# Query features and x of three groups in full-depth matmuls with block diagonal matrices, and an earlier masked multiplication for z

## The chip, the cores and the metric

The kernel runs on one core of a Trainium2 chip. The metric is the device time of one execution in microseconds (us), as a median over runs. The engines are named as the profile does: PE is TensorE (matmuls), PEld its weight loads, DVE is VectorE, ACT is ScalarE, POOL is GpSimd, SP is SyncE, whose queue starts most of the DMAs.

## The reference, cut to what matters

```
def phi(x):                                   # r = 8
    a = einsum('rd,bhsd->bhsr', S1, x)
    b = einsum('rd,bhsd->bhsr', S2, x)
    return einsum('bhsi,bhsj->bhsij', a, b)   # 64 features
kv  = einsum('bhsf,bhsd->bhfd', phi(k), v)
z   = sum_s phi(k)
x   = (phi(q) @ kv) / (phi(q) . z + 1e-6)     # 4 batches, 4 heads, 1088 rows, 32 columns
x   = x transposed to (4352, 128)             # heads side by side
h   = x @ w_in                                # 128 -> 2048
g   = where(h > 0, h, exp(min(h, 0)) - 1)     # ELU
out = g @ w_out                               # 2048 -> 128
```

All is computed in fp32. The weights arrive as 64-bit words and are rounded on the chip.

## The kernel before, in words

The 4352 rows are cut into 9 groups: eight of 512 rows (two to a batch) and group 8, the last 64 rows of each of the four batches (256 rows). The groups 4 and 5, and 6 and 7, are handled as pairs up to x.

The order of all work is written out by hand. After an opening part, a loop runs over steps n = 2 to 63. A step belongs to a group and to one of eight pairs of 128-column blocks of the hidden layer. In it PE computes `h` (`mm1`, at L256: two blocks, 512 rows; up to step 29 each product is four matmuls that are 32 columns wide, from step 30 two that are 64 wide), ACT and DVE make the ELU of both blocks (`elu`: L808 and L810 on ACT, L816 on DVE), and PE runs the second product of step n-2 (L256 for group 0, L713 for most of group 1, and from step 16 on a scheme of seven products of quarter blocks at L737, for which POOL adds up ELU results at L696 to L701). Calls that are hung on a step by hand stand in lists: `at(n, ...)` after mm1 of step n, `mid(n, ...)` after the first block's ELU, `late(n, ...)` after the second's. Each engine works through its instructions in that order.

Hung on the steps are the key side of batches 1 to 3 and the query side of groups 2 to 8:

- `KF_late` (L359) computes the key features of a batch into two banks `kfps`, `KF_late_out` (L369) turns them, `KO_a` (L378) copies one factor to PSUM (tile `ka`) and `KO_b` (L386) multiplies, `KA` (L427) sums kv and z into one bank `kv`. `sums_out` copies z's part (`ZC`, L444) and turns kv (`KT_out`, L436), which stores it to DRAM and loads it back in four copies (`kvs`, L439 and L440). `turn` multiplies z's part with a matrix on PE (`Z`), `turned` multiplies it with a mask on DVE (`Z_out`, L453) and adds heads together on POOL (`Z_share`, L458 and L459) into `SWs`.
- `queries(g5, g1, n)` (L655) computes x of a group (`q5`, L642) and the features of a later one (`q1`, L536), in 32x32 tiles of the array: 16 matmuls for the features, two times 16 for x. They write four banks: the two `h` banks of the next step and two `aux` banks (`qps`). `q1_out` (L548) turns four pieces on DVE, `q5_out` (L653) copies four pieces on ACT. `q2_den` (L560 to L570) makes the quotient, `q2_half` (L625) the outer product, `q4` (L632) turns it.

PSUM has four banks for `h` (two steps), two for everything with the tag `aux`, used in turn, and one each for the two outputs. A tile with tag `aux` waits for the readers of the tile that had its bank.

```
    for n, g, nx in ((13, None, 2), (15, 2, 3), (22, 3, 4), (30, 4, 6), (46, 6, 8), (62, 8, None)):
        at(n, queries, g, nx, n + 1)
```

So x of group 3 and the features of group 4 stand in step 22, and so on. The key side of batch 2 has `KF_late` in step 16, `KA` in 19 and z in 20; that of batch 3 has `KF_late` in 21, `KO_b` in 23 and 24, `KA` in 27 and z in 28.

Of the kernel before, what the change touches and what calls it, by code (L numbers as in the profile page):

```python
# [12 lines left out]
F32 = mybir.dt.float32  # L13
# [9 lines left out]
def _ap(ap: bass.AP, free):  # L23
    return dataclasses.replace(ap, ap=[list(ap.ap[0])] + [list(x) for x in free])
# [3 lines left out]
def kernel(  # L28
# [21 lines left out]
    nc = tc.nc  # L50
    B, H, S, D = q.shape
    R = S1.shape[0]
    P = 128
    FD = H * D
# [3 lines left out]
    NT = S // 64  # L58
# [5 lines left out]
    const = ctx.enter_context(tc.tile_pool(name="const", bufs=1))  # L64
    work = ctx.enter_context(tc.tile_pool(name="wk", bufs=2))
    psum = ctx.enter_context(tc.tile_pool(name="psum", bufs=2, space=bass.MemoryType.PSUM))
# [6 lines left out]
    qT = [const.tile([FD, NT, 64], F32, name=f"qT{b}") for b in range(2)] * 2  # L73
    qE = const.tile([FD, 2, 64], F32, name="qE")
# [162 lines left out]
    bmask = const.tile([FD, H], F32, name="bmask")  # L237
# [15 lines left out]
    def quarters(dst, lhs, rhs, tile=None, **kw):  # L253
        tile = tile or width[0]
        for c in range(0, P, tile):
            nc.tensor.matmul(dst[c:c + tile], lhs[:, c:c + tile], rhs, skip_group_check=True,  # L256
                             tile_position=(0, c), **kw)
# [36 lines left out]
    Sab = const.tile([FD, H, 2 * R], F32, name="Sab")  # L294
    SW = const.tile([FD, H, 3, R], F32, name="SW")
# [16 lines left out]

    def make_SWs():
        nc.gpsimd.memset(SWs[:, :, 3, :], 0.0)
        for b in range(B):
            nc.gpsimd.tensor_add(SWs[:, b, :2, :], Sxp[:, :, 0, :], Sxp[:, :, 1, :])


# [5 lines left out]


    kvS = const.tile([P, H, D], F32, name="kvS")
    kvs = {b: const.tile([P, H, 2, D], F32, name=f"kvs{b}") for b in range(B)}
    dram = ctx.enter_context(tc.tile_pool(name="dram", bufs=1, space=bass.MemoryType.DRAM))
    kvd = {b: dram.tile([P, 2 * D], F32, name=f"kvd{b}")[:] for b in range(B)}
    kv_ps, feats, wzs, kf_ps = {}, {}, {}, []  # L330


# [99 lines left out]

    def KT_out(b):

        kt = work.tile([P, 2 * D], F32, name="kvt", tag="kvt")
        nc.vector.transpose(kt[:], kv_ps[b][:, :R * R])  # L436
        nc.sync.dma_start(kvd[b], kt[:])
        src = kvd[b].rearrange("(h p) x -> p h x", h=H)
        for w in range(4 if b else 1):  # L439
            nc.sync.dma_start(kvs[b][32 * w:32 * w + 32].rearrange("p h f d -> p h (f d)"), src)  # L440

    def ZC(b, ps):
        zl = work.tile([P, H * R], F32, name="zl", tag="zl")
        nc.scalar.copy(zl[:], ps[:, R * R:R * R + H * R])  # L444
        return zl
# [3 lines left out]
        quarters(ps[:, 96:128], SXh[:], zl[:], None if b else 64)  # L449

    def Z_out(b, ps):
        z = wzs[b] = SW[:, :, 2, :] if b == 0 else work.tile([FD, H, R], F32, name="wz", tag="wz")[:]
        nc.vector.tensor_mul(z, ps[:, 96:128].rearrange("p (h i) -> p h i", h=H), _ap(bmask[:], [[1, H], [0, R]]))  # L453

    def Z_share(b):
        z = wzs.pop(b)
        zh = work.tile([FD, 2, R], F32, name="zh", tag="zh")
        nc.gpsimd.tensor_add(zh[:], z[:, :2], z[:, 2:])  # L458
        nc.gpsimd.tensor_add(SWs[:, b, 2, :], zh[:, 0], zh[:, 1])  # L459
# [14 lines left out]
    NQ = (NH + 7) // 8  # L474
    qn = [min(8, NH - 8 * g) // 2 for g in range(NQ)]
    abw, ans, qp, qpT, xg, xps = {}, {}, {}, {}, {}, {}
# [7 lines left out]
    def half_tile(g, k):  # L484
        return (g // 2, 8 * (g % 2) + k) if g < NQ - 1 else (k, NT - 1)
# [36 lines left out]
    units = {g: ([g, g + 1] if 4 <= g < NQ - 1 else [g]) for g in [2, 3] + list(range(4, NQ, 2))}  # L522
    un = {g: sum(qn[x] for x in gr) for g, gr in units.items()}

    def quarter_of(g, w):

        n = un[g] // 2
        return (*half_tile(g + n * w // 8, n * w % 8), n)

    def q1(g, ps, o, opened):  # L530
        for w in range(4):
            b, t, n = quarter_of(g, w)
            qs = qE[:, b:b + 1, :] if g == NQ - 1 and b < 2 else qT[b][:, t:t + n, :]
            for r in range(4):
                rows = slice(32 * r, 32 * r + 32)
                nc.tensor.matmul(ps[r][32 * w:32 * w + 32, o:o + 64 * n], SWs[rows, b].rearrange("p x r -> p (x r)"),  # L536
                                 qs[rows].rearrange("p t s -> p (t s)"),
                                 start=not opened, stop=True, skip_group_check=True, tile_position=(32 * r, 32 * w))
        abw[g] = ps, o

    def q1_out(g):
        (ps, o), n = abw[g], un[g]
        pair = n > 4
        abw[g] = work.tile([P, H * n if pair else H * 4, 4 * R], F32, name="abw", tag="abwp" if pair else "abw",
                           bufs=1 if pair else 2)
        m = H * n // len(ps)
        for r in range(len(ps)):
            nc.vector.transpose(abw[g][:, m * r:m * r + m, :].rearrange("p m y -> p (m y)"),  # L548
                                ps[r][:, o:o + 32 * m])
# [97 lines left out]
    def q5_out(g, i=0):  # L647

        n = 32 * un[g]
        ps = xps[g] if len(units[g]) == 1 else xps[g][2 * i:2 * i + 2]  # L650
        x = xg[g + i] = work.tile([P, 512], F32, name="xg", tag="xg", bufs=3)
        for w in range(len(ps)):
            nc.scalar.copy(x[:, n * w:n * w + n], ps[w][:, :n])  # L653

    def queries(g5, g1, n):  # L655

        hs[steps[n]] = [psum.tile([P, 512], F32, name="h", tag="h", bufs=4) for c in range(2)]
        ps = hs[steps[n]] + [psum.tile([P, 512], F32, name="qps", tag="aux") for _ in range(2)]
        if g5 is not None:
            q5(g5, ps, 0)  # L660
        if g1 is not None:
            q1(g1, ps, 256 if g5 is not None else 0, g5 is not None)
        if g5 is not None:
            q5(g5, ps, 1)
# [236 lines left out]
    KO_first(5, 7)  # L901
    Z(0, zps, zl)
    Z_out(0, zps)
    KO_first(7, KT)
    keep_warm(1, 96, 64)
# [52 lines left out]
    def at(n, f, *a):  # L958
        extra.setdefault(n, []).append((f, *a))

    def mid(n, f, *a):
        extra.setdefault((n, 0), []).append((f, *a))

    def late(n, f, *a):
        extra.setdefault((n, 1), []).append((f, *a))
# [8 lines left out]
    late(3, keep_last, 0)  # L974
    late(14, keep_last, 1)
    late(2, make_SWs)
    late(3, Z_share, 0)
    late(3, KT_out, 0)
    zls = {}

    def sums_out(b):
        zls[b] = ZC(b, kv_ps[b])
        KT_out(b)
# [3 lines left out]

    def turned(b):
        Z_out(b, kv_ps[b])
        Z_share(b)  # L990


    for b, (n_t, n_f, n_o, n_a, n_z) in enumerate(
            ((4, 6, (7, 9), 11, 12), (15, 16, (17, 18), 19, 20), (19, 21, (23, 24), 27, 28)), 1):
        at(n_t, transp, kT, "k", b, 0, NT)
        at(n_f, KF_late, b)
        late(n_f, KF_late_out, b)
        for half in range(2):
            if b == 1:
                at(n_o[half], KO, b, half, nc.gpsimd)  # L1000
            else:
                late(n_o[half] - 1, KO_a, b, half)
                at(n_o[half], KO_b, b, half)
        at(n_a, KA, b)
        late(n_a, sums_out, b)
        at(n_z, turn, b)
        late(n_z, turned, b)
    late(10, transp, qT, "q", 1, 0, NT)
    at(21, transp, qT, "q", 2, 0, NT)
    late(24, transp, qT, "q", 3, 0, NT)  # L1010

    for n, g, nx in ((13, None, 2), (15, 2, 3), (22, 3, 4), (30, 4, 6), (46, 6, 8), (62, 8, None)):
        at(n, queries, g, nx, n + 1)
        if g is not None:
            mid(n, q5_out, g)
        if nx is not None:
            mid(n, q1_out, nx)
        if g is not None and len(units[g]) > 1:
            late(n, q5_out, g, 1)
# [3 lines left out]
    late(19, q2_den, 3)  # L1023
    late(19, q2_half, 3, 0)
    late(20, q4, 3)
    late(22, q2_den, 4)
    for n, g, i in ((25, 4, 0), (26, 4, 1), (32, 6, 0), (35, 6, 1)):
        late(n, q2_a, g, i)
    at(26, q2_half, 4, 0)
# [17 lines left out]
    for n in range(2, N):  # L1047
        g, cp = steps[n]
# [29 lines left out]
        g, cp = before  # L1078
# [10 lines left out]
    g = NQ - 2  # L1089
# [53 lines left out]
```

## Time and profile before

| | |
|---|---|
| median of 3 runs | 264.51 us (264.0 to 264.83) |
| span of the profiled execution | 262.8 us |
| what lies around the span, against the median | 1.7 us |
| PE busy | 256.6 us (98%) |
| DVE, ACT, POOL busy | 188.4, 183.0, 169.4 us |
| chain that ended last | PE 93% |
| x of a group and features (`h`, `qps` at L642, and `h` at L536), of the chain | 1.4%, 0.8%, 0.7% |

The span is the time from the first to the last instruction of one profiled execution. Times of single instructions are from that execution. The chain is followed back from the last instruction: at each step to what released it, or to the instruction before it on its engine. An instruction's row gives its start, its length, its engine and line, what it writes and reads and, in brackets, the idle time of the engine before it and what ended that. Lengths on one engine overlap a little: two DVE rows of 0.68 us take 1.27 us together.

### The profile page before, as it was taken

The numbers are of one execution on the slowest core, as the hardware profiler recorded it, in microseconds if no ns is written. First come the engines' busy times: TensorE is split into PE (matmuls) and PEld (weight loads), VectorE is DVE, ScalarE is ACT, GpSimd is POOL, SyncE is SP. The second block draws the span as 40 slices with busy tenths as digits, with TensorE's granted clock in tenths as the row PEclk, the third lists the DMA queues.
The fourth block names the chain that finished last, engine by engine and source line by source line (L and its number), as shares of the span: only waits on it lengthen the run. The fifth ranks groups of instructions, "written<-read, shape, count | busy, mean of one in ns | idle before, by whom it ended". The sixth has DMA issues, their size and how long they took to land.

```text
span 262.8 us, 9940 instructions
## 1 busy us (share of the span) xinstructions
PE 256.6 (98%) x4219; PEld 159.2 (61%) x4219; DVE 188.4 (72%) x355; ACT 183.0 (70%) x356; POOL 169.4 (64%) x253
## 2 busy tenths in 40 slices
PE   8899999999999999999999999999999999999994
PEld 6652333354446756667666666665666666667994
DVE  6799999997969997997477676644456445664651
ACT  2469878667567647785687777776777777777792
POOL 4420008204587996798868799898689888997310
PEclk9999999999999999999999999999999999999999
DMA  6999079012012220001100200011001100110021
GB/s 167 315 360 224 12 229 253 28 34 81 12 19 30 31 39 5 5 15 29 32 0 4 30 13 2 0 29 15 5 0 18 26 4 0 20 23 5 2 30 33
DMA packets 28507, 14.30 MB, mean 54 GB/s; under 512 B 21392, under 2 KB 26640, under 8 KB 28464
## 3 DMA queue, kind: packets, MB, share of 16 engines
q1 hardware_dynamic: 28032, 13.32, 21.2%
q8 instruction: 33, 0.54, 0.9%
q10 hardware_dynamic: 368, 0.30, 0.3%
q14 instruction: 10, 0.08, 0.1%
q0 software_dynamic: 64, 0.07, 0.1%
HBM read 11.31 MB, written 2.36 MB: 52 GB/s over the span
## 4 chain that ended last, share of the span: by engine, by line
PE 93%; DMA 2%; DVE 1%; ACT 1%; SPq 0%; issue 0%; DVEq 0%
PE h L256 44%; PE pb L737 16%; PE pa L737 13%; PE o L256 5%; PE pb L713 4%; PE ol L256 3%; DMA hd_q<-in_q_dram 2%; PE h L642 1%; PE kv L427 1%; PE kfps L359 1%; PE qps L642 1%; PE h L536 1%; PE qtp L595 1%; DVE qp L583 0%; PE xps L602 0%; PE qps L536 0%
## 5 line engine op out<-in xcount | busy, mean ns | idle before, releaser
L256 PE MATMUL h<-xg,W 128*32 128x512 f32 (+3 forms) x904 | 131.0, 540 | 0.4 <-ACT xg L608 0.4
L816 DVE SCALAR_TENSOR_TENSOR gg<-e,h 128x512 f32<-128x512 f32 x128 | 85.5, 681 | 54.2 <-ACT e L810 50.7
L808 ACT ACTIVATE e<-h 128x512 f32<-128x512 f32 x128 | 75.5, 590 | 47.4 <-PE h L256 46.5
L810 ACT ACTIVATE e<-e 128x512 f32<-128x512 f32 x128 | 80.9, 632 | 3.8
L256 PEld LDWEIGHTS h<-xg,W 128*32 128x32 f32 (+1 forms) x904 | 43.2, 122 | 43.1 <-issue 33.5
L699 POOL TENSOR_TENSOR tt<-gg 128x256 f32<-128x256 f32 x50 | 36.9, 738 | 15.6 <-DVE gg L816 15.2
L701 POOL TENSOR_TENSOR tt<-gg,tt 128x256 f32<-128x256 f32 x50 | 38.0, 761 | 3.9
L696 POOL TENSOR_TENSOR tt<-gg 128x256 f32<-128x256 f32 x50 | 36.7, 735 | 5.6 <-DVE gg L816 5.2
L700 POOL TENSOR_TENSOR tt<-tt,gg 128x256 f32<-128x256 f32 x50 | 36.6, 732 | 3.9
L737 PEld LDWEIGHTS pa<-gg,W 128*64 128x64 f32 (+1 forms) x496 | 24.0, 126 | 23.7 <-issue 23.0
L737 PE MATMUL pa<-gg,W 128*64 128x128 f32 (+1 forms) x496 | 30.7, 274 | 0.0
L737 PE MATMUL pb<-tt,SS 128*64 128x128 f32 (+1 forms) x480 | 29.7, 273 | 0.0
L737 PEld LDWEIGHTS pb<-tt,SS 128*64 128x64 f32 (+1 forms) x480 | 22.9, 126 | 0.0
L737 PE MATMUL pa<-tt,SS 128*32 128x128 f32 (+1 forms) x288 | 21.2, 273 | 0.0
L737 PE MATMUL pb<-tt,W 128*64 128x128 f32 (+1 forms) x256 | 20.2, 273 | 0.0
L737 PE MATMUL pb<-gg,SS 128*64 128x128 f32 (+1 forms) x256 | 20.0, 273 | 0.0
L134 POOL TENSOR_TENSOR raw<-raw,tiny 128x512 f32<-128x512 f32 x1 | 1.0, 1044 | 24.7 <-DVE raw L129 24.7
L256 PE MATMUL o<-gg,W 128*32 128x512 f32 x128 | 15.3, 595 | 0.0
L737 PEld LDWEIGHTS pa<-tt,SS 128*32 128x32 f32 (+1 forms) x288 | 13.8, 124 | 0.0
L737 PEld LDWEIGHTS pb<-tt,W 128*64 128x64 f32 (+1 forms) x256 | 12.9, 125 | 0.1
L737 PEld LDWEIGHTS pb<-gg,SS 128*64 128x64 f32 (+1 forms) x256 | 12.8, 125 | 0.0
L713 PE MATMUL pb<-gg,W 128*32 128x256 f32 x192 | 11.6, 380 | 0.0
(154 smaller groups left out, 285.0 us busy)
## 6 DMA issues: line engine op xcount, KB each, us to landing
raw<-in_moe_w_in_dram SPq DMA_DIRECT2D x8, 256.0 KB, 6.5
raw<-in_moe_w_out_dram SPq DMA_DIRECT2D x8, 256.0 KB, 6.6
out_dram<-ob SPq DMA_DIRECT2D x112, 16.0 KB, 1.5
hd_k<-in_k_dram SPq DMA_DIRECT2D x3, 544.0 KB, 7.6
hd_q<-in_q_dram SPq DMA_DIRECT2D x3, 544.0 KB, 8.8
v<-in_v_dram SPq DMA_DIRECT2D x4, 288.0 KB, 7.6
v<-in_v_dram SPq DMA_DIRECT2D x4, 256.0 KB, 8.9
kvs<-kvd SPq DMA_DIRECT2D x13, 32.0 KB, 2.0
```

The source lines that it names most:

```text
L256: nc.tensor.matmul(dst[c:c + tile], lhs[:, c:c + tile], rhs, skip_group_check=True, tile_position=(0, c), **kw)
L359: nc.tensor.matmul(ps[g2][32 * c:32 * c + 32, :32 * KT], Sxp[r].rearrange("p x c r -> p (x c r)"), kT[b][r, u * KT:u * KT + KT, 32 * w:32 ...
L642: nc.tensor.matmul(ps[w][32 * r:32 * r + 32, :64 * n], kvs[b][rows, r, f, :], qpT[g, i][rows, o:o + 2 * n, f, :], start=(f == 0), stop=(f ...
L696: nc.gpsimd.tensor_tensor(t[:, 0], b12, b11, op=SUB)
L699: nc.gpsimd.tensor_tensor(t[:, 2], b22, b12, op=SUB)
L700: nc.gpsimd.tensor_tensor(t[:, 1], t[:, 2], b11, op=ADD)
L701: nc.gpsimd.tensor_tensor(t[:, 3], b21, t[:, 1], op=SUB)
L713: nc.tensor.matmul(acc[1][0][r:r + width[0], 256 * hi:256 * hi + 256], lhs[:, w:w + width[0]], gg[:, c, 256 * u:256 * u + 256], start=(cp ...
L737: nc.tensor.matmul(bank[r:r + width[0], P * col:P * col + P], lhs[:, w:w + width[0]], rhs[:, u], start=(first and i in ((0,) if g == 1 els ...
L808: nc.scalar.activation(e, hs[g, cp][c][:, :n], RELU, scale=-1.0)
L810: nc.scalar.activation(e, e, EXP, scale=-1.0)
L816: nc.vector.scalar_tensor_tensor(gs[g, cp][:, c, :n], es[g, cp][:, c, :n], -1.0, hs[g, cp][c][:, :n], op0=ADD, op1=MAX)
```

## The change

For the groups 2, 3 and 8 the query features and x are computed with all 128 rows of the array: `SWd` holds, for each batch, the features' matrix with the heads on the diagonal, and `kvb` holds kv in the same way, built by a multiplication of the turned kv with the mask (`KT_wide`) in SBUF, so that batches 0 and 1 no longer go through DRAM. `q1_wide` and `q5_wide` write one `aux` bank each, 512 columns (256 for group 8), and one transposition (`q1_wide_out`) and one copy (`q5_wide_out`) empty them. The features of group 4 go from step 22 to step 23, with their quotient. `turned` is hung on the step with `at` and no longer with `late`, so the mask multiplication stands ahead of both ELU steps on DVE, and POOL's addition of heads remains for batches 2 and 3.

```diff
     def make_SWs():
         nc.gpsimd.memset(SWs[:, :, 3, :], 0.0)
+        nc.gpsimd.memset(SWd[:, :, :, 3, :], 0.0)
         for b in range(B):
+            nc.gpsimd.tensor_copy(SWd[:, b, :, :2, :], Sab[:].rearrange("p h (x r) -> p h x r", x=2))
+        nc.gpsimd.tensor_copy(SWd[:, 0, :, 2, :], SW[:, :, 2, :])
+        for b in range(2, B):
             nc.gpsimd.tensor_add(SWs[:, b, :2, :], Sxp[:, :, 0, :], Sxp[:, :, 1, :])
...
     def KT_out(b):
-        kt = work.tile([P, 2 * D], F32, name="kvt", tag="kvt")
-        nc.vector.transpose(kt[:], kv_ps[b][:, :R * R])
-        nc.sync.dma_start(kvd[b], kt[:])
+        kt = kts[b] = work.tile([P, 2, D], F32, name="kvt", tag="kvt")
+        nc.vector.transpose(kt[:].rearrange("p f d -> p (f d)"), kv_ps[b][:, :R * R])
+        if b < 2:
+            return
+        nc.sync.dma_start(kvd[b], kt[:].rearrange("p f d -> p (f d)"))
         src = kvd[b].rearrange("(h p) x -> p h x", h=H)
-        for w in range(4 if b else 1):
+        for w in range(4):
             nc.sync.dma_start(kvs[b][32 * w:32 * w + 32].rearrange("p h f d -> p h (f d)"), src)
+
+    def KT_wide(b, eng):
+        eng.tensor_mul(kvb[:, b], _ap(kts.pop(b)[:], [[D, 2], [0, H], [1, D]]), _ap(bmask[:], [[0, 2], [1, H], [0, D]]))
...
     def Z_out(b, ps):
-        z = wzs[b] = SW[:, :, 2, :] if b == 0 else work.tile([FD, H, R], F32, name="wz", tag="wz")[:]
+        z = wzs[b] = SWd[:, b, :, 2, :] if b else SW[:, :, 2, :]
...
+    def tiles_of(g):
+        if g < NQ - 1:
+            b, t = half_tile(g, 0)
+            return [(b, qT[b][:, t:t + 8, :], 0, 512)]
+        return [(k, qE[:, k:k + 1, :] if k < 2 else qT[k][:, NT - 1:NT, :], 64 * k, 64) for k in range(B)]
+
+    def q1_wide(g):
+        p = psum.tile([P, 512], F32, name="qps", tag="aux")
+        for b, x, o, n in tiles_of(g):
+            quarters(p[:, o:o + n], SWd[:, b].rearrange("p h x r -> p (h x r)"), x.rearrange("p t s -> p (t s)"),
+                     start=(o == 0), stop=True)
+        abw[g] = p
+
+    def q1_wide_out(g):
+        m, p = H * un[g], abw[g]
+        abw[g] = work.tile([P, H * 4, 4 * R], F32, name="abw", tag="abw", bufs=2)
+        nc.vector.transpose(abw[g][:, :m, :].rearrange("p m y -> p (m y)"), p[:, :32 * m])
+
+    def q5_wide(g):
+        p = psum.tile([P, 512], F32, name="xps", tag="aux")
+        for f in range(2):
+            for b, x, o, n in tiles_of(g):
+                quarters(p[:, o:o + n], kvb[:, b, f].rearrange("p h d -> p (h d)"),
+                         qpT[g, 0][:, o // 32:(o + n) // 32, f, :], start=(f == 0 and o == 0), stop=(f == 1))
+        xps[g] = p
+
+    def q5_wide_out(g):
+        n = qn[g] * P
+        xg[g] = work.tile([P, 512], F32, name="xg", tag="xg", bufs=3)
+        nc.scalar.copy(xg[g][:, :n], xps.pop(g)[:, :n])
...
-    late(3, Z_share, 0)
     late(3, KT_out, 0)
+    late(3, KT_wide, 0, nc.gpsimd)
...
     def turned(b):
         Z_out(b, kv_ps[b])
-        Z_share(b)
+        if b > 1:
+            Z_share(b)
...
         late(n_a, sums_out, b)
+        if b == 1:
+            late(n_a, KT_wide, b, nc.gpsimd)
+        else:
+            late(36 + b, KT_wide, b, nc.vector)
         at(n_z, turn, b)
-        late(n_z, turned, b)
+        at(n_z, turned, b)
...
-    for n, g, nx in ((13, None, 2), (15, 2, 3), (22, 3, 4), (30, 4, 6), (46, 6, 8), (62, 8, None)):
+    for n, g in ((13, 2), (15, 3), (46, 8)):
+        at(n, q1_wide, g)
+        mid(n, q1_wide_out, g)
+    for n, g in ((15, 2), (22, 3), (62, 8)):
+        at(n, q5_wide, g)
+        mid(n, q5_wide_out, g)
+    for n, g, nx in ((23, None, 4), (30, 4, 6), (46, 6, None)):
         at(n, queries, g, nx, n + 1)
...
-    late(22, q2_den, 4)
+    late(23, q2_den, 4)
```

More of the change, by code (lines that the diff above doesn't have):

```diff
@@ L326 @@
     kvS = const.tile([P, H, D], F32, name="kvS")
-    kvs = {b: const.tile([P, H, 2, D], F32, name=f"kvs{b}") for b in range(B)}
+    kvs = {b: const.tile([P, H, 2, D], F32, name=f"kvs{b}") for b in range(2, B)}
+    kvb = const.tile([P, B, 2, H, D], F32, name="kvb")
+    SWd = const.tile([FD, B, H, 4, R], F32, name="SWd")
+    kts = {}
     dram = ctx.enter_context(tc.tile_pool(name="dram", bufs=1, space=bass.MemoryType.DRAM))
-    kvd = {b: dram.tile([P, 2 * D], F32, name=f"kvd{b}")[:] for b in range(B)}
+    kvd = {b: dram.tile([P, 2 * D], F32, name=f"kvd{b}")[:] for b in range(2, B)}
     kv_ps, feats, wzs, kf_ps = {}, {}, {}, []
@@ L532, in q1 @@
             b, t, n = quarter_of(g, w)
-            qs = qE[:, b:b + 1, :] if g == NQ - 1 and b < 2 else qT[b][:, t:t + n, :]
+            qs = qT[b][:, t:t + n, :]
             for r in range(4):
@@ L649, in q5_out @@
         n = 32 * un[g]
-        ps = xps[g] if len(units[g]) == 1 else xps[g][2 * i:2 * i + 2]
+        ps = xps[g][2 * i:2 * i + 2]
         x = xg[g + i] = work.tile([P, 512], F32, name="xg", tag="xg", bufs=3)
```

## The prediction

> **What bounds the kernel now.** I read the page's busy shares and its chain first, then the chain in order of time, which gives the start of every step, then the waits, then the timelines of VectorE (DVE) and ScalarE (ACT) around the places that the change touches. A step n is: the eight matmuls into `h` (mm1), what is hung on it, and the second product (mm2) of step n-2.
>
> Busy shares and the chain by engine:
>
> ```profile
> PE 256.6 (98%) x4219; PEld 159.2 (61%) x4219; DVE 188.4 (72%) x355; ACT 183.0 (70%) x356; POOL 169.4 (64%) x253
> PE 93%; DMA 2%; DVE 1%; ACT 1%; SPq 0%; issue 0%; DVEq 0%
> ```
>
> TensorE (PE) is the chain, and its granted clock is 1.00 in the stretches around the change. So what counts is PE's time per step, plus each stretch in which PE waits. From the chain in order of time (start, length, piece), starts of steps 13, 14, 15, 16, 17, then 19 to 24:
>
> ```profile
> 61.88 1.72 PE h L256 x16
> ...
> 65.91 1.72 PE h L256 x16
> 67.62 1.72 PE o L256 x16
> 69.34 1.72 PE h L256 x16
> ...
> 74.50 1.72 PE h L256 x16
> ...
> 78.53 1.72 PE h L256 x16
> ...
> 85.02 1.72 PE h L256 x16
> ...
> 89.46 1.68 PE h L256 x14
> ...
> 92.77 0.90 PE h L256 x8
> ...
> 97.53 1.72 PE h L256 x16
> ...
> 102.74 1.72 PE h L256 x16
> ...
> 105.98 1.72 PE h L256 x16
> ```
>
> A plain step is 3.43 us up to step 15 (65.91 to 69.34: 1.72 + 1.71) and 3.25 after it (102.74 to 105.98). What a step takes beyond that is its block of query or key matmuls, or a wait. Same view, steps 46 and 47, 62 and 63:
>
> ```profile
> 181.10 1.72 PE h L256 x8
> ...
> 186.23 1.72 PE h L256 x8
> ...
> 234.90 1.72 PE h L256 x8
> ...
> 239.08 1.72 PE h L256 x8
> ```
>
> The wait that the change's last words aim at, and three rows of DVE's timeline (start, length, instruction, idle time before it) that I use below:
>
> ```profile
> PEld kfps L359 <- DVE wz L453: 0.6, 1, 0.6
> ```
>
> ```profile
> 98.55 0.82 DVE L369 STREAM_TRANSPOSE abk<-kfps 128x288 f32<-128x288 f32 x2
> 105.66 1.48 DVE L386 TENSOR_TENSOR kp<-ka,abk 128x1280 f32<-128x1280 f32 x1
> 183.35 0.69 DVE L816 SCALAR_TENSOR_TENSOR gg<-e,h 128x512 f32<-128x512 f32 x1 [1.47 <-ACT e L810]
> ```
>
> **Matmuls, step by step.** What the present blocks cost beyond a plain step: step 13 4.03 - 3.43 = 0.60; step 15 5.16 - 3.43 = 1.73; step 22 5.21 - 3.25 = 1.96; step 46 5.13 - 3.25 = 1.88; step 62 4.18 - 3.25 = 0.93. Step 30, which stays, runs 126.97 to 132.42: 2.20 for 48 matmuls of 256 columns. About 0.14 of each is paid by the matmuls behind it (the `pb` piece after step 13 takes 1.87, not 1.73).
>
> The new blocks have exactly the shape of mm1: four matmuls, 128 rows deep, 32 columns wide, 512 streamed. Eight of those take 1.72, so one set is 0.86. The features of a group are one set, its x two.
> - Step 13, features of 2: 0.86 for 0.60, **+0.26**.
> - Step 15, features of 3 and x of 2: 2.58 for 1.73, **+0.85**.
> - Step 22, x of 3: 1.72 for 1.96, **-0.24**.
> - Step 23 gets the features of group 4 alone, 16 small matmuls of 256 columns, which step 22 loses: a third of step 30's block is 0.73; at most 0.87 if the 0.14 is paid in full. I take **+0.80**, since it is a block by itself.
> - Step 46: x of 6 is two thirds of 2.20, 1.47; features of 8 are eight matmuls 64 wide on 64 columns. Bounds: 0.44 by the last stage's rate (four 64-wide on 128 columns, 0.44) and 0.68 by eight such matmuls at 8.34 (`abqp`). I take 0.50, as the array is already streaming: 1.97 for 1.88, **+0.09** (up to +0.27).
> - Step 62, x of 8: sixteen of those, 0.88 to 1.36; I take 1.00 for 0.93, **+0.07** (-0.05 to +0.43).
>
> Sum **+1.83** (1.55 to 2.4).
>
> Beside the row for step 13 (sixteen matmuls of 128 columns in 32x32 tiles, 0.60) stands a rule that speaks against this change: "TensorEngine Tiling (Array Packing)" in the Trainium skill, overview, gives up to 16 times for 32x32 tiles, because all sixteen run side by side. By it, as an estimate, step 13's block would cost a quarter of a set, 0.21, the five present blocks 2.9 and not the 7.1 of the rows, and the change would add 5 us of matmuls, not 1.8. The rows decide.
>
> **The z multiplication.** Step 16 holds the same `kfps` block as step 21 without a wait: 78.53 - 74.50 = 4.03 against 97.53 - 92.77 = 4.76. The second half of step 21's block waits for a bank that `Z_out` of batch 2 frees. That instruction goes from behind both ELU steps of step 20 to ahead of them, to 93.7 + shift, before the block is reached. The wait of 0.73 goes, **-0.73** (0.5 to 0.73). The ELU steps behind it lose 0.1 on a queue that is not yet waited for. In step 28 DVE idles 1.5 us at that point, and step 12 feeds no block that waits now: nothing there.
>
> **What is late next.** The `aux` tag has two banks, used in turn, and the change alters the turns.
> - Step 22. x of 3 takes the bank of the first `kfps`, freed by the first of the transpositions at 98.55 (so 98.98). DVE shows no idle time from 82 to 99.4 and keeps its work, which starts from PE's step 17; so it moves by what steps 13 and 15 add, 1.11, to 100.1. PE comes to it at 97.53 + 1.11 - 0.73 + 1.72 = 99.63. Wait **+0.46** (0 to 0.7): most of the z gain goes back to DVE.
> - Step 23. The features of group 4 need both banks; the second holds `KO_a` of batch 3 until the multiplication at L386 has read it. Behind x of 3 (ends 101.85) ACT copies 0.6, does the second ELU half (1.2) and the 0.29 copy into the bank, to 104.0; DVE does `gg` (0.6) to 104.4 and the 1.48 product, to 105.85. PE is there at 101.85 + 1.53 + 1.72 = 105.1. Wait **+0.75** (0 to 1.0). All of PE's queue stands behind it: the small matmuls, mm2, mm1 of step 24.
> - Step 46 allocates three `aux` tiles at two banks: the fourth small matmul of x of 6 needs the bank of group 8's features, which frees after their transposition on DVE, behind `gg`. Counted from the step's start: `gg` begins at 183.35 - 181.10 = 2.25, occupies 0.6, then 0.41 for 128x256 (the row at L548) and a handover: 3.3. PE is there at 1.72 + 0.50 + three small issues, 2.3. Wait **+1.0** (0.8 to 1.3).
> - Step 27 now is 120.41 - 115.72 = 4.69, where step 19 with the same block takes 4.44 (89.46 - 85.02). PE will come over 2 us later and DVE's work in steps 23 to 26 not: **-0.25** (0 to -0.25).
>
> The rest is covered. GpSimd (POOL) gets 5 small copies, a memset and two 128x256 products (each about 0.75, as the `tt` rows), and loses 6 small additions; it sits idle 24.7 and 15.0 us in the waits of those stretches. `weights7` starts earlier, no longer behind the z of batch 1. SP's queue loses two stores and five loads. DVE has one 0.71 transposition for four of 0.27 twice, and two more products of about 0.35 in steps 38 and 39, where it idles over 1 us a step. If that cover failed, each would cost its own length.
>
> **Sum.** 1.83 - 0.73 + 0.46 + 0.75 + 1.0 - 0.25 = **+3.1 us**. The profiled span is 262.8, 1.7 under the median of 264.51; I expect a span near 265.9 and 264.5 + 3.1 = **267.6**. With the low ends +1.3, with the high ends +5.
>
> **Rivals.**
> 1. The bank waits of steps 22 and 23 fall away because DVE gets ahead of PE: +1.9, 266.4; without that of 46 too, +0.9, 265.4. For: the turns of 22 and 23 hang on sums of a dozen DVE and ACT rows, each known to 0.1. Against: step 46's does not. Chance 0.20.
> 2. DVE falls further behind. The feature transposition of group 4 (four of 0.4) and its quotient (2 us) move one step later, while `q2_half` stays in step 26; if DVE then loses a full step, an `h` bank is missed in step 25 or 26: 1 to 2 us more, 269. Against: my running sum leaves DVE 0.1 to 2 us of room there. Chance 0.13.
> 3. Faster: a wide set costs much less than mm1's. With no new wait at all the sum is +0.85; to be 0.8 us under the present (0.3%, about what a measurement of this kernel can tell from no change) six sets must give 1.65, so it decides under 0.58 us a set. Against: every step up to 29 has two sets of that very shape at 0.86. At that price the time is 263.7. Chance 0.04; between, no change, 0.04.
>
> My forecast has 0.59. The range takes in rival 1 and half of rival 2: 265.4 to 269.2. Faster 0.04, same 0.04, slower 0.92.
>
> **What would show it.** Right: step 13 near 4.3, step 15 near 6.0, step 21 near 4.0; a gap on PE before `xps` in step 22, before the fourth small matmul of step 23 with DVE L386's product as releaser, and in step 46 with the 128x256 transposition. Wrong: a step 15 under 5.5 (the set's price), no gap in 46 (the banks' turns), or new gaps in steps 24 to 29 (rival 2).

## The result and the profile after

The changed kernel takes 268.3 us (median of 4 runs, 268.18 to 268.66), beside 264.5 us for the kernel before: a ratio of 1.0148, 95% interval 1.0136 to 1.016. It is slower by 3.8 us; the prediction said 3.1, with 267.6 for the time. The span of the profiled execution is 266.6 us, 3.8 above the 262.8 of before and again 1.7 under the median.

Busy shares and the chain by engine, from the page of the changed kernel:

```profile
PE 259.7 (97%) x4027; PEld 158.9 (60%) x4027; DVE 188.7 (71%) x348; ACT 182.5 (68%) x347; POOL 170.6 (64%) x255
PE 90%; DVE 6%; ACT 2%; issue 1%; DVEq 0%
```

PE has 192 instructions fewer and is busy 3.1 us longer. DVE's share of the chain has gone from 1% to 6%: PE now waits for DVE at places where it did not wait before. Half of the 6% (8 us) is one stretch from 41 to 50 us, which the chain goes through on DVE because of a single wait of 0.20 at its end; the three waits named below have 3.6 us of DVE's rows.

The chain of the changed kernel in order of time (start, length, piece), where the prediction named a step:

```profile
62.08 1.78 PE h L256 x16
...
66.45 1.72 PE h L256 x16
...
69.88 1.72 PE h L256 x16
71.60 0.86 PE qps L256 x8
72.46 1.72 PE xps L256 x16
...
75.89 1.72 PE h L256 x16
...
94.17 1.72 PE h L256 x16
...
98.19 0.90 PE h L256 x8
...
100.03 0.40 DVE abk L376
...
100.47 1.97 PE xps L256 x16
...
104.93 1.41 DVE kp L393
...
106.38 0.40 PE qps L548
...
108.75 1.72 PE h L256 x16
...
183.69 0.88 PE h L256 x4
...
186.63 0.37 DVE abw L569
...
187.05 0.40 PE qps L685
...
190.18 1.72 PE h L256 x8
...
238.85 1.72 PE h L256 x8
...
243.03 1.72 PE h L256 x8
```

The rows of `h` start steps 13, 14, 15, 16, 21, 22, 24, 46, 47, 62 and 63. A set of four matmuls is 0.86 (`qps` in step 15; the trace has two records for each matmul, so x8 is a set), two sets are 1.72 (`xps`). The DVE rows in the chain are the three waits: a key transposition (`abk`) ahead of x of 3, the key product (`kp`) ahead of the small matmuls of step 23, and the 128x256 transposition (`abw`) in step 46. The differences of these starts, beside those of before:

| stretch | before, us | after, us | difference | predicted |
|---|---|---|---|---|
| ahead of step 13 | 61.88 | 62.08 | +0.20 | 0 |
| step 13 | 4.03 | 4.37 | +0.34 | +0.26 |
| step 15 | 5.16 | 6.01 | +0.85 | +0.85 |
| step 21 | 4.76 | 4.02 | -0.74 | -0.73 |
| steps 22 and 23 | 8.45 | 10.56 | +2.11 | +1.77 |
| step 26 | 3.25 | 3.35 | +0.10 | 0 |
| step 27 | 4.69 | 4.42 | -0.27 | -0.25 |
| step 46 | 5.13 | 6.49 | +1.36 | +1.09 |
| step 62 | 4.18 | 4.18 | 0 | +0.07 |
| from step 63 on | 23.72 | 23.57 | -0.15 | 0 |
| sum | | | +3.80 | +3.06 |

The plain stretches between (steps 31 to 45, 47 to 61) have the same length to 0.01 us in both. The last row of the table does not come from the matmuls: from step 63 to the last row of `ol` on PE the two chains take 18.10 and 18.09, and the rest hangs on what follows the matmuls and on the rounding of the spans.

### The profile page after: what moved, and what is told of

Its sections match the earlier page's. It is cut to its first block, busy times and chain, and to the rows that moved or that the text cites. A ratio compares the mean times of both kernels' runs of the same rounds, so it can differ in the third digit from the quotient of the medians.

```text
span 266.6 us, 9530 instructions
## 1 busy us (share of the span) xinstructions
PE 259.7 (97%) x4027; PEld 158.9 (60%) x4027; DVE 188.7 (71%) x348; ACT 182.5 (68%) x347; POOL 170.6 (64%) x255
## 4 chain that ended last, share of the span: by engine, by line
PE 90%; DVE 6%; ACT 2%; issue 1%; DVEq 0%
PE h L256 41%; PE pb L780 16%; PE pa L780 13%; PE o L256 5%; PE pb L756 3%; PE ol L256 3%; PE xps L256 2%; DVE gg L859 1%; PE idle L264 1%; PE kv L434 1%; DVE raw L121 1%; PE abp L347 1%; PE kfps L366 1%; ACT e L851 1%; PE qps L256 1%
## 5 line engine op out<-in xcount | busy, mean ns | idle before, releaser
L256 PEld LDWEIGHTS h<-xg,W 128*32 128x32 f32 (+1 forms) x904 | 42.6, 122 | 43.6 <-issue 35.0
L452 POOL TENSOR_TENSOR kvb<-kvt,bmask 128x256 f32<-128x256 f32 x2 | 1.9, 974 | 27.0 <-DVE kvt L443 27.0
```

## The experiments

Each is an edit of the kernel before or after. Ratios are against the kernel before, with 95% intervals.

**The z multiplication alone**, in the kernel before:

```
-        late(n_z, turned, b)
+        at(n_z, turned, b)
```

> The kernel before with one edit: the masked multiplication for z ahead of the ELU steps. My theory (the z gain is given back to DVE at once): step 21 falls from 4.76 to about 4.03 us, but PE then reaches step 22's block at 98.5 and its banks still come free from the transpositions at 98.98 and 99.4, so step 22 grows by the same 0.7; total 0.0 (-0.15 to +0.1), 264.5. Rival (the wait was real and nothing follows): -0.7, 263.8.

Measured: 264.39 us, ratio 0.9998 (0.9984 to 1.0011). Steps 22 and 23 of its chain start at:

```profile
96.14 1.72 PE h L256 x16
...
102.11 1.72 PE h L256 x16
```

Step 21 begins at 92.11, so it takes 4.03, the 0.73 are saved; but step 22 takes 5.97 where it took 5.21, 0.76 more. PE comes to the next bank that DVE has not freed yet, that much sooner. Its waits in that stretch show it (total us, number, longest):

```profile
PEld qps L642 <- DVE abk L369: 0.5, 2, 0.3
```

The gain of step 21 is given back in full in the very next step. A smaller one stays: step 15 takes 4.99 where it took 5.16, here and in the two other profiled versions in 32x32 tiles that have the early multiplication. The time does not show it: the interval includes no change.

**Group 8's features two steps earlier**, in the changed kernel, so that step 46 allocates two `aux` tiles and not three:

```
-    for n, g in ((13, 2), (15, 3), (46, 8)):
+    for n, g in ((13, 2), (15, 3), (44, 8)):
```

> The changed kernel with the features of group 8 in step 44 instead of 46, so that step 46 books two aux banks and not three. Theory (bank turn): step 46 falls from 6.49 to about 4.7 (3.25 and two thirds of step 30's 2.20), step 44 grows by 0.44; together -1.3, 267.0. Rival (the wait moves to the banks of step 44 or to ACT): 0 to -0.3, 268.1.

Measured: 267.08 us, ratio 1.0092 (1.0077 to 1.0107), span 265.4. Its steps 46 and 47 start at:

```profile
184.06 1.72 PE h L256 x8
...
188.88 1.72 PE h L256 x8
```

Step 46 is 4.82, not 6.49; step 44 is 3.71, its plain 3.25 and 0.46 for the eight matmuls. So the wait in step 46 cost 6.49 - 4.82 - 0.46 = 1.21 us, and the span fell by 1.2. The two banks and their turns are shown to be its cause.

**A set doubled**: the features of group 3 are issued twice in step 15 of the changed kernel.

```
 def q1_wide(g):
     p = psum.tile([P, 512], F32, name="qps", tag="aux")
+    if g == 3:
+        for b, x, o, n in tiles_of(g):
+            quarters(p[:, o:o + n], SWd[:, b]..., x..., start=(o == 0), stop=True)
```

> The changed kernel with the feature matmuls of group 3 in step 15 issued twice into the same bank: four more matmuls, 128 rows deep, 32 wide, 512 columns. Theory (PE sets the end and a set is 0.86): +0.86 against the changed kernel, 269.2. Rival (part of a set is covered, since DVE sets the pace in steps 17 to 22): +0.0 to +0.4, 268.5.

Measured: 269.1 us, ratio 1.0179 (1.0166 to 1.0192), 0.8 us above the changed kernel. In its chain the second set is added at full price; the next step starts at 76.75, not 75.89:

```profile
71.60 1.72 PE qps L256 x16
...
76.75 1.27 PE h L256 x10
```

So the price of a set is on the path, and rival 3 (a set under 0.58) falls.

**The key products of batch 3 one step later**, in the changed kernel:

```
-  (19, 21, (23, 24), 27, 28)), 1):
+  (19, 21, (24, 25), 27, 28)), 1):
```

> The changed kernel with both halves of the key product of batch 3 (copy into the bank, multiplication) one step later, so that step 23's features find both aux banks free. Theory: the gap of 0.7 before the fourth small matmul and the restart after it go, -0.7 to -0.9, 267.5. Rival (DVE has no room one step later): the product now stands beside the outer products of group 4 in steps 25 and 26, and a wait for an h bank of 0.3 to 0.7 appears in steps 25 to 28; total 0 to -0.4, 268.1.

Measured: 269.3 us, ratio 1.0179 (1.0164 to 1.0194): slower still. Steps 22 and 23 take 9.60 and not 10.56, the gap ahead of the small matmuls of step 23 is gone. But from step 26 on the chain shows:

```profile
114.19 0.90 PE h L256 x8
...
117.83 0.27 DVE cc L818
...
118.24 1.08 PE pb L780 x32
119.32 1.72 PE h L256 x16
```

Step 26 takes 5.13. In it the second product begins a new output, for which `cc` on DVE must first empty the bank; DVE comes to that behind the product that was moved. The wait was moved by three steps and grew.

**The kv product of batch 0 on DVE, late in step 16**, in the changed kernel, to take POOL's product out of the opening part:

```
-    late(3, KT_wide, 0, nc.gpsimd)
+    late(16, KT_wide, 0, nc.vector)
```

> The changed kernel with the block diagonal kv of batch 0 built on DVE in step 16, where DVE idles, and not on POOL in step 3. Theory (POOL's 0.98 product at 30.2 lengthens the DVE instruction beside it by 0.26, and DVE is what step 8 waits for): step 8 starts 0.2 earlier, total -0.2, 268.1. Rival (the 0.2 ahead of step 13 is a difference between executions): 0.0, 268.3.

Measured: 268.42 us, ratio 1.0145 (1.0127 to 1.0162). Step 13 starts at 61.73, so the opening part is as short as before; but step 18 takes 3.61 in place of 3.25: the product took 0.79 on DVE there and stands ahead of the key work and of the sums that empty an output bank. That this is what PE waits for is read from DVE's rows; the profile itself names an ELU row of ACT.

**The same product in step 40**, where DVE idles (a third `kvt` buffer keeps the data until then):

```
-    kt = kts[b] = work.tile([P, 2, D], F32, name="kvt", tag="kvt")
+    kt = kts[b] = work.tile([P, 2, D], F32, name="kvt", tag="kvt", bufs=3)
-    late(3, KT_wide, 0, nc.gpsimd)
+    late(40, KT_wide, 0, nc.vector)
```

> The changed kernel with the block diagonal kv of batch 0 built on DVE in step 40, where DVE idles over 1 us a step, from a third buffer; POOL's product at 30.2 is gone. Theory (that product lengthens a DVE instruction beside it, and step 8 waits for DVE): step 13 starts 0.2 to 0.35 earlier and nothing is lost in step 18, total -0.2 to -0.35, 268.1. Rival: 0.0, 268.4, as in the run with step 16.

Measured: 268.07 us, ratio 1.0135 (1.012 to 1.0151), span 266.3. Step 9 takes 3.45, as in the kernel before, and not 3.65: the opening wait is gone. What that is worth in time is not shown. The intervals of the two ratios overlap; of the 0.3 by which the span is shorter, 0.28 lies ahead of the moved product, since this execution comes to its first `h` row at 15.83 us and that of the changed kernel at 16.11; and PE, which comes sooner, takes 4.72 in step 19 where it took 4.45, and 10.17 in steps 22 and 23 together where it took 10.56.

**All the waits taken out together**, in the changed kernel: features of 8 in step 44, key products in (24, 25), the kv product late in step 16, and

```
-    at(21, transp, qT, "q", 2, 0, NT)
+    mid(22, transp, qT, "q", 2, 0, NT)
```

> The changed kernel with all its new waits taken away: features of group 8 in step 44, the key product of batch 3 one step later, the transposition of q of batch 2 from ahead of step 21's ELU on DVE to the middle of step 22 (so that the key transpositions come 1.26 earlier and free the bank for x of group 3), and kv of batch 0 on DVE in step 16. Theory: what is left is the price of the matmuls, 1.8, less the z wait, 0.73, and the wait of step 27, 0.27: 0.7 to 0.9 above the kernel before, 265.3. Rival A (the waits are not the cause, the wide matmuls cost more than their rows say): over 266.5. Rival B (wide sets are free once nothing waits): at or under 264.3.

Measured: 267.48 us, ratio 1.012 (1.0107 to 1.0133). Steps 22, 23 and 24 start at:

```profile
98.15 1.72 PE h L256 x16
...
103.11 1.72 PE h L256 x16
...
107.15 1.72 PE h L256 x16
```

Steps 22 and 23 take 4.96 and 4.04, together 9.00, which is what the prediction's matmul terms make without waits (8.45 - 0.24 + 0.80 = 9.01). So the two waits cost 10.56 - 9.00 = 1.56 us. But steps 25 and 26 take 8.39 for 6.5: the output bank again, 1.9 us. A miss, because of that.

**The same with DVE relieved ahead of step 26**: the kv product in step 40 and

```
-    late(24, transp, qT, "q", 3, 0, NT)
+    late(28, transp, qT, "q", 3, 0, NT)
```

> The run with the new waits taken away, once more, with the transposition of q of batch 3 in step 28 instead of 24 (DVE idles there, and step 30 is the first to need it) and kv of batch 0 on DVE in step 40. Theory (what that run lost, 1.8, is the wait of step 26 for the output banks at the change from group 2 to 3, which DVE empties behind the moved key product and this transposition): -1.8 and -0.2 or more against it, 265.4; that is the price of the matmuls, 1.8, less 0.73 and 0.27 against the kernel before. Rival (the wide matmuls cost more): over 266.5.

Measured: 265.9 us, ratio 1.0056 (1.0044 to 1.0068). Steps 25 and 26 take 7.15, 0.65 above plain. What is left of the change then is 265.9 - 264.5 = 1.4 us: 0.65 for this wait and 0.8 for the rest, and 1.83 - 0.73 - 0.27 is 0.83, the matmuls less the two gains. That these agree so well is in part luck: by its steps this version still loses 0.14 in step 19 (4.58 for 4.44) and keeps 0.62 of the 0.73 in step 21 (4.14 for 4.76). The matmul terms themselves are there without waits: +0.85 in step 15 (6.01), 9.00 in steps 22 and 23. So the matmuls are slower by themselves, apart from all waits.

**The narrow blocks kept**: the kernel before with the z multiplication early, x of 3 and the features of 4 in step 23, and the key products in (24, 25).

```
-  (19, 21, (23, 24), 27, 28)), 1):
+  (19, 21, (24, 25), 27, 28)), 1):
...
-        late(n_z, turned, b)
+        at(n_z, turned, b)
...
-  (22, 3, 4)
+  (23, 3, 4)
...
-    late(22, q2_den, 4)
+    late(23, q2_den, 4)
```

> The kernel before, all blocks in 32x32 tiles, with z's masked multiplication ahead of the ELU steps, the block with x of 3 and features of 4 in step 23 instead of 22, and the key product of batch 3 one step later. Theory (the z gain is kept once no block waits for the key transpositions): -0.7 to -0.9 against the kernel before, 263.7, faster than both. Rival (step 24 waits for the copies of x, which it needs at once): step 24 starts 0.3 to 0.8 late, total -0.4 to +0.2.

Measured: 265.54 us, ratio 1.0038 (1.0024 to 1.0052), a miss. Which of its steps lost the time was not read.

**The same with the transposition of q of batch 3 in step 28** (as above):

> The kernel before in 32x32 tiles with z ahead of the ELU steps, the block of step 22 in step 23, the key product of batch 3 one step later, and the transposition of q of batch 3 in step 28 instead of 24. Theory (the output banks of step 26 come free in time): -0.7 to -1.2 against the kernel before, 263.5, faster than both. Rival (step 24 or 26 still waits): 264.3 to 265.

Measured: 264.31 us, ratio 0.9988 (0.9979 to 0.9996), span 262.6: the only version whose interval lies under the kernel before, by 0.12%. Steps 21, 22 and 23 take 4.03, 3.24 and 5.01, so the 0.73 is kept there; 0.78 goes again in steps 25 and 26 (7.28), for the output bank, and 0.38 in step 27 (5.07 for 4.69), whose second product PE starts 0.44 late; the profile names no releaser. Mostly a miss: 263.5 was expected.

**DVE's work of steps 24 to 26 moved back by half a step or one**, in that version, and in the experiment behind it the same three moves on the changed kernel without its waits:

```
-    at(25, KO_b, 3, 1)
+    late(25, KO_b, 3, 1)
...
-    at(26, q2_half, 4, 0)
-    late(26, q2_half, 4, 1)
+    late(26, q2_half, 4, 0)
+    late(27, q2_half, 4, 1)
```

> The last narrow run, with the second key product of batch 3 behind the output transposition of step 25 instead of ahead of its ELU, and the two outer products of group 4 half a step and one step later. Theory (the wait of 0.65 to 0.8 that is left in steps 25 and 26 is for the output banks, which DVE empties behind that product): steps 25 and 26 go back to 6.5 together, -0.7 against the last narrow run, 263.6, 0.9 under the kernel before. Rival (the product only moves the wait to an h bank in step 28): 0.0 to -0.3, 264.2.

Measured: 265.6 us, ratio 1.0045 (1.0032 to 1.0059). Steps 25 and 26 are down to 6.5, as without a wait; step 27 takes 6.87 for the 5.07 of the version without the moves. The list of waits has two new entries (total us, number, longest):

```profile
PE kv L427 <- DVE qp L625: 1.3, 1, 1.3
...
PE pb L737 <- POOL tt L699: 0.7, 1, 0.7
```

`KA` of batch 3 needs an `aux` bank whose reader is the outer product that was moved; the second product of the same step waits for one of POOL's sums. On the changed kernel without its waits:

> The same three moves in the wide kernel with its waits taken away. Theory: -0.65, 265.3; what is then left above the kernel before, 0.75, is the matmuls' price of 1.83 less the waits that went in steps 21 (0.73) and 27 (0.27). Rival: 0.0 to -0.2, 265.8, and a wait of that size in step 28.

Measured: 266.77 us, ratio 1.0088 (1.0074 to 1.0102), step 27 5.88. `KA` starts at 119.91, 0.11 after the same outer product ends (the profile names an ACT row that ended at 119.61), so the cause is in all likelihood the same; and step 28 takes 3.85 where it took 3.31, the wait that the rival named. Both missed.

## Why the prediction was right, and by what it was off

- **The price of a set** (0.86) was exact: step 15 has +0.85, and the doubled set makes that step 0.86 longer and costs 0.8 us of time. Of step 13's +0.34, 0.26 is as forecast and 0.06 the first `h` row (1.78 for 1.72).
- **The z gain**: -0.74 in step 21, for -0.73. That it goes back to DVE was said of most of it; alone, all of it goes back. That step 12 feeds no block that waits was wrong: in the kernel before, the earlier multiplication saves 0.17 in step 15 (in the rows, POOL's weight sums, L685, have then moved away from beside DVE's quotient, and `L570` takes 0.29 there and not 0.50; this was not tested by itself). The 1.73 that the prediction took there for the price of matmuls holds a wait of that size. The difference of +0.85 stands, because the changed kernel has no wait in that step (3.43 + 3 x 0.86 = 6.01).
- **The three waits** are at the three places named, with the releasers named. They carried the mis-sized term: 0.46 + 0.75 + 1.0 = 2.21 was forecast, and by the versions without them they cost 1.56 + 1.21 = 2.77. The idle times of PE that the profile shows are smaller than either: 0.56, 0.19 and 0.62. It counts them from the modelled end of the matmul before, and matmuls overlap: those of `h` are 0.59 long, and in an unbroken row the next ones start 0.43 after them (1.72 / 4). Timelines of PE in steps 22 and 23, the changed kernel:

```profile
98.01 1.90 PE L256 MATMUL h<-xg,W 128*32 128x512 f32 x16
100.47 1.92 PE L256 MATMUL xps<-qpT,kvb 128*32 128x512 f32 x16 [0.56 <-DVE abk L376]
102.21 0.29 PE L780 MATMUL pa<-gg,W 128*32 128x128 f32 x4
...
105.57 0.41 PE L548 MATMUL h<-qT,SWs 32*32 32x256 f32 x2
...
106.38 0.40 PE L548 MATMUL qps<-qT,SWs 32*32 32x256 f32 x1 [0.19 <-DVE kp L393]
```

and in step 22, the second version without the waits:

```profile
97.67 1.90 PE L256 MATMUL h<-xg,W 128*32 128x512 f32 x16
99.39 1.90 PE L256 MATMUL xps<-qpT,kvb 128*32 128x512 f32 x16
101.11 0.62 PE L780 MATMUL pa<-gg,W 128*32 128x128 f32 x16
```

From the start of `h` to the start of x of 3 it is 2.46 with the wait and 1.72 without, so 0.74 is lost, not 0.56; x itself takes 1.74 to the next start, for 1.72. In step 23 three small matmuls are still running when the wait begins: the fourth starts 0.81 after the first, without the wait 0.02. In step 46 it starts 1.24 after the first (187.05 and 185.81). By the lengths of the steps the three waits cost 0.77, 0.79 and 1.21. The prediction's working for step 22 set the release of the bank against the end of `h` in the chain, 0.16 after the next matmul would have started; the bank also came free 0.1 later, against that end, than worked out. Its 0.46 is the term that was most off. Step 23 (0.75) was nearly right. In step 46 (1.0) the release came 0.06 later than in the working, 3.36 after the step's start, and PE was there a little sooner.
- **"The rest is covered"** is the step that failed outright, by 0.20. The kv product of batch 0 on POOL (0.98, where about 0.75 was expected) lies in idle time of POOL, as stated, but beside work of DVE. Timeline of DVE, the kernel before:

```profile
30.76 0.45 DVE L121 TENSOR_SCALAR raw<-raw 128x512 uint32<-128x512 uint32 x1
...
59.39 0.43 DVE L121 TENSOR_SCALAR raw<-raw 128x512 uint32<-128x512 uint32 x1
```

Timelines of DVE, POOL and PE, the changed kernel:

```profile
30.71 0.71 DVE L121 TENSOR_SCALAR raw<-raw 128x512 uint32<-128x512 uint32 x1
...
59.60 0.73 DVE L121 TENSOR_SCALAR raw<-raw 128x512 uint32<-128x512 uint32 x1
...
61.10 0.69 DVE L137 SCALAR_TENSOR_TENSOR W<-raw,W 128x512 f32<-128x512 f32 x1
...
30.17 0.98 POOL L452 TENSOR_TENSOR kvb<-kvt,bmask 128x256 f32<-128x256 f32 x1 [15.76 <-DVE kvt L443]
...
59.07 0.97 POOL L452 TENSOR_TENSOR kvb<-kvt,bmask 128x256 f32<-128x256 f32 x1 [11.20 <-DVE kvt L443]
...
50.30 1.92 PE L256 MATMUL h<-xg,W 128*32 128x512 f32 x16 [0.20 <-DVE gg L859]
```

The same instruction takes 0.26 longer beside POOL's 0.98, and PE, which in the kernel before went into step 10 without idling, waits 0.20 for DVE 20 us later (the expectations of the two experiments on it call this step 8). With the product out of the opening part, `L121` takes 0.44 and step 9 is 3.45 again, so the cause of this wait is shown. The product of batch 1 on POOL does the same at 59.60, 0.30 over the kernel before. `L137`, which rounds weights, comes later by it, and step 13 loads its first weights 0.12 after `L137` ends, in both kernels; the first `h` row of that step is 1.78 here and 1.81 to 1.89 in the other versions of the changed kernel. No version moved this product, so that part is read from the rows and not tested. "GPSIMD Engine Reference" in the Trainium skill, section "1. Specifications", says that POOL's SBUF interfaces are shared with VectorE; it gives no amount, and whether `L121` runs in the form that it names for contention is shown by no run here.

- **Off by little**: step 62 cost nothing where +0.07 was expected, the matmuls of step 46 cost 0.15 and not 0.09 (3.71 + 4.82 - 3.25 - 5.13), and step 26 has +0.10; for the last there was no experiment. All terms together: 0.20 in the opening, 0.56 for the three waits, and the small ones cancel.
- **The rivals.** Rival 1 (the bank waits of 22 and 23 fall away) did not come about in the changed kernel, and its price for them was 1.2 us, where 1.56 is measured. Rival 2's mechanism, DVE late for a bank in steps 25 and 26, is real: it came up in each version that moved the key product there, with an output bank in place of an `h` bank, until further moves took the wait to step 27. In the changed kernel itself, those steps show +0.10 in all. Rival 3 fell with the doubled set.

What stays open: which order of DVE's work in steps 22 to 28 keeps the 0.73 of step 21. Three orders gave it back in step 22, in steps 25 and 26, or in step 27, as each wait taken out showed the next bank.

## What to carry to other kernels

Price a removed wait by what is late next: here the 0.73 us of a wait taken out came back as 0.76 a step later, because the same engine owed PE another bank there. When a schedule written by hand changes the number of tiles in a tag, write down whose readers each turn waits for; that gave the places and the releasers of the three new waits, and the cost of each within about 0.3 us. Count a wait of PE from the start that the next matmul would have had, and not from the end that the profile gives to the one before: 0.19 us shown as idle stood for 0.79 lost. And count an instruction on an idle engine as covered only if its neighbour on the other engines has time to spare too.

## What the runs showed of the hardware

At a granted clock of 1.00, PE lost next to nothing by starting anew: behind an idle time of 0.56 us, the eight matmuls of x took 1.74 us from their first start to the next row's, and 1.72 without a wait. A DVE instruction of 128x512 words (`L121`), 0.43 to 0.45 us by itself, took 0.71 and 0.73 beside a POOL product of 0.98, and 2.07 beside two POOL products that take 4.96 together (in the changed kernel at 46.09; before, the same 2.07), although the profile shows no wait of one for the other. Each time it ended 0.27 to 0.29 us after POOL did, whether POOL had 0.44 or 1.78 us left when it started. `L117`, which had begun shortly before POOL's product of 0.98, took 0.66 and 0.67, for 0.64 and 0.65 without one.
